# Reordering the start-up, the linear-memory path and the recurrent path of a two-path attention kernel

## The chip, the cores and the metric

The kernel runs on one core of one Trainium2 chip. The metric is the device time of one execution in microseconds. A run whose matmul clock is low throughout and whose time is more than 1.5% above the fastest of the same kernel counts as slow and is left out of every comparison; there is one such run here, the profiled one of `after_again` (1854.24 us at a mean clock of 0.707).

The engines are named as the profile names them: PE (matmuls), PEld (PE's weight loads), DVE (vector engine), ACT (activation engine), POOL, SP (here it only issues DMAs).

## The reference

Two attention paths read the same `x` (2048 x 512, bf16) and a sigmoid gate mixes them.

```python
def _A_ref(x, mem0, Wq, Wk, Wv, Wo, seg_len):      # 32 heads of 128, seg_len 32, memory of 8 rows
    mem = mem0
    for s in range(S // seg_len):                  # 64 segments, one after the other
        h = concat([mem, x[segment s]])            # 40 rows
        q, k, v = h @ Wq, h @ Wk, h @ Wv           # per head
        p = softmax(mask(q k^T * scale))
        o = (p v) @ Wo
        mem = o[:, :8]; outs.append(o[:, 8:])      # the memory feeds the next segment

def _B_ref(x, wq, wk, wv, wo, beta):               # 32 heads of 16, 4 blocks of 512 rows
    for s in range(4):
        a_dot = softmax(causal(q k^T * scale)) v
        a_mem = (phi(q) M) / (phi(q) z + 1e-6)     # phi(t) = t+1 if t > 0 else exp(t)
        o = g * a_mem + (1 - g) * a_dot            # g = sigmoid(beta), one number per head
        M += phi(k)^T v; z += sum(phi(k))
    return o @ wo

g = sigmoid((x * gate_w).sum(-1))
return g * _A_ref(...) + (1 - g) * _B_ref(...)
```

## The kernel before

The kernel records operations with what they read and write, per engine, and turns the dependences into semaphore waits. Each engine is given its own list, in the recorded order, and the order in which operations are planned is what this change alters. Three parts run one after the other: start-up, path B, path A.

Start-up: four weight loads share one semaphore group, and DVE pads wq and wk ahead of the evictions of the transposed x.

```python
        P.dma(g_bw, ... wqN_sb ...); P.dma(g_bw, ... wkN_sb ...); P.dma(g_bw, ... wvB_sb ...)   # [cut]
        for nat, pad, rn, rp in ((wqN_sb, wqB_sb, "wqN", "wqB"), (wkN_sb, wkB_sb, "wkN", "wkB")):
            P.op("dve", ... dv.memset(pad[:], 0.0) ...)
            for c in range(C):
                P.op("dve", ... dv.tensor_copy(pad[...][:, :, 0:DH], nat[...]) ...)
    P.dma(g_bw, ... woB_sb ...)
    # [cut] transposes of x on PE, each evicted to xT by DVE
```

Path B works on groups of 4 heads, 8 groups in each of 4 blocks. A group has 10 score tiles per head in three waves ("w"; 4, 4 and 2 tiles), each followed by exponentials on ACT; the K, Q, V projections and phi(K) ("pKr") of the next group are put in between, and PV ("p"), the linear memory's numerator ("nz"), its update ("mz") and a DVE chain that mixes both belong to the group before.

```python
        seq = []                                # order in one pass of the loop over groups, before
        if havew: seq.append(("w", 0))
        if havep: seq.append(("mz", None)); seq.append(("p", qc_parts[0]))
        if haven: seq.append(("pK", None))
        if havew and NW > 1: seq.append(("w", 1))
        if havep and len(qc_parts) > 1: seq.append(("p", qc_parts[1]))
        if haven: seq.append(("pQ", None))
        # [cut] ("w", 2)
        if havep: seq.append(("nz", None))
        if haven: seq.append(("pV", None))
        if havep: seq.append(("chain", None))
        if haven: seq.append(("pKr", None))
        # [cut]
    # phi(K): PE product -> DVE kmin -> ACT kexp -> DVE phik; kp, projQ and mz share PSUM bank 7
    # chain, blocks 1 to 3: rd, ad, dm, rm, am, df = am-ad, dg = df*g, o = ad+dg   (8 DVE operations)
```

Path A, one segment: K and Q projections, scores, exponentials, mask, normalisation, V projection, transposes of P, PV, Wo.

```python
    # at the start of segment s: the memory, from the bank of the last Wo (behind the eviction "atx" of aT)
        P.op("dve", lambda dv: dv.tensor_copy(hTc[:, :, SEG:L], src), reads=[rbank[6]], writes=[rm], name="hm%d" % s)
    # [cut] K, Q (evicted by ACT), scores
    tr_after = {4: 0, 6: 1, 7: 2}               # P transposes of head groups 0, 1, 2 after V groups 4, 6, 7
    # [cut] groups 0 and 1 transpose into bank 0, group 2 into bank 1
    pend = v["A_pending_tail"]
    if pend:                                    # every fourth segment: 4 transposes of aT, 4 B-row matmuls
        plan_group_tail_pe(pend[0], ...)
    P.op("dve", ... PT_sb[0:L, 0:24 * L] <- bank 0 ...)
    P.op("dve", ... PT_sb[0:L, 24 * L:H * L] <- bank 1 ...)
    # [cut]
    vres = [Rs("V_sb%d" % j) for j in range(NVC)]
    for b, (h0, h1) in enumerate(HG):           # PV: every group waits for all of V
        P.op("pe", f_pv, reads=vres + ptres, writes=[rbank[b]], ...)
        P.op("act", ... OT_sb[...] <- bank b ...)
    # [cut] Wo, then atx
```

The softmax here doesn't subtract the row's maximum and nothing guards it: scores larger than these inputs give would overflow.

## Time and profile before

| | before |
|---|---|
| median of 5 runs (range) | 1854.98 us (1848.8 to 1857.86) |
| span of the profiled run, mean granted clock | 1853.8 us, 0.884 |
| first projection of path B (start of its weight load) | 31.1 us |
| period per group, blocks 0 / 1 and 2 / 3 | 8.4 (6.9 to 9.7) / 13.9 / 10.1 us |
| path A, mean period of a segment | 22.19 us |

A period is the distance between the same instruction in neighbouring passes, read from the timeline (for block 0 the eviction of V).

The table by stretches of the kernel before; the stretches are the start-up, blocks 0 to 3 of path B (cut at each block's first projection), the stretch that waits for Wv and Wo, and path A from its first Wo matmul on. Columns: stretch, its length, busy time and count of PE, PEld, DVE, ACT and POOL, then granted clock, DMA share, GB/s.

```profile
0.00:31.10 31.10, 8.60 (x133) 7.95 (x134) 13.02 (x30) 1.92 (x4) 3.67 (x12) 0.76 0.94 351
31.10:109.00 77.90, 52.29 (x1091) 32.91 (x1107) 36.97 (x100) 46.08 (x105) 20.30 (x32) 0.78 0.06 24
109.00:221.00 112.00, 64.80 (x1219) 42.21 (x1233) 58.55 (x159) 49.32 (x112) 20.30 (x32) 0.62 0.01 2
221.00:333.40 112.40, 64.70 (x1219) 41.64 (x1233) 58.27 (x158) 49.29 (x112) 20.30 (x32) 0.62 0.01 2
333.40:422.00 88.60, 57.30 (x962) 33.97 (x974) 48.84 (x112) 46.81 (x104) 21.23 (x34) 0.63 0.01 1
422.00:447.19 25.19, 20.48 (x384) 14.56 (x385) 5.17 (x12) 10.11 (x19) 2.09 (x4) 0.79 0.95 335
447.19:1853.80 1406.61, 1325.83 (x32496) 1016.42 (x32512) 375.54 (x852) 666.12 (x1262) 117.60 (x250) 0.95 0.02 5
```

In blocks 1 and 2 no engine is busy more than 58% of the time, so they are bound by waits. In path A PE is busy 94%.

The waits of the kernel before: who waited for whom, microseconds in total, times, longest.

```profile
ACT Kmin L545 <- DVE Kmin L543: 76.1, 24, 5.0
...
PE pb L634 <- DVE phiKg L547: 52.4, 21, 3.3
...
PE pb L618 <- DVE phiQ L508: 38.4, 18, 2.3
...
PE pb L796 <- DVE hT L785: 30.4, 63, 0.5
```

The first line is the key to path B. The timeline of one group of block 2 shows it (start, length, engine, line, operation, and in brackets the idle time before it and what ended it):

```profile
248.13 0.43 DVE L675 TENSOR_TENSOR orow<-adot,dtmp 128x256 bf16<-128x256 f32 x1
248.48 0.42 DVE L543 TENSOR_SCALAR Kmin<-pb 128x256 bf16<-128x256 f32 x1
248.93 0.42 ACT L545 ACTIVATE Kmin<-Kmin 128x256 bf16<-128x256 bf16 x1 [4.52 <-DVE Kmin L543]
...
249.25 2.04 ACT L580 ACTIVATE PT_g<-pb 128x512 bf16<-128x512 f32 x4
```

The score matmuls of this wave started at 245.92 and took 0.64 us, so their exponentials (L580) could have begun near 246.6. They began at 249.25, because on ACT they stand behind the phi(K) exponential (L545), whose input DVE makes only after the chain that ends with L675. In these lines ACT did not start the ready exponentials ahead of the waiting operation: of the 4.52 us in which it stood idle, about 2.3 passed with them ready behind it (246.6 to 248.93).

In path A the interesting place lies between V and Wo. The chain of waits of one segment of the kernel before (start, length, what):

```profile
...
1044.18 0.60 ACT V_sb L868
...
1044.83 0.48 PE pb L894 x12
...
1045.39 0.58 ACT OT_sb L899
...
1046.02 4.35 PE pb L908 x128
...
1050.39 0.29 DVE aT_st L914
1050.68 0.11 DVE hT L785
...
1050.84 1.17 PE pb L796 x40
```

PV (L894) waits for the last V eviction on ACT; Wo (L908) waits for the first PV eviction; the next segment's K (L796) waits for two DVE operations, of which only the second makes its input. Wo takes 4.35 us here and 3.4 to 3.6 us in segments without half clock. The difference is the clock, by half-microsecond stretches of the same segment:

```profile
1046.50:1047.00 0.50, 0.50 (x20) 0.50 (x20) 0.00 (x0) 0.25 (x1) 0.00 (x0) 1.00 0.00 0
1047.00:1047.50 0.50, 0.50 (x24) 0.50 (x20) 0.00 (x0) 0.00 (x0) 0.00 (x0) 0.66 0.00 0
1047.50:1048.00 0.50, 0.50 (x21) 0.50 (x18) 0.00 (x0) 0.00 (x0) 0.00 (x0) 0.50 0.00 0
...
1050.50:1051.00 0.50, 0.16 (x7) 0.17 (x7) 0.28 (x2) 0.00 (x0) 0.00 (x0) 0.93 0.00 0
```

From 1047.15 to 1050.57 the granted clock (third number from the end) is 0.50. The numbers in brackets count every matmul that is under way in a stretch, so they don't show the pace; the starts do: of two Wo matmuls in a row, the second starts 25 ns after the first at full clock and 33 ns at half clock (medians of this trace). This spell lasts 3.4 us. In stretches of half a microsecond, path A has 40 such spells.

### The profile page before, as it was taken

How to read it: one execution, taken by the hardware profiler on the slowest of the kernel's cores; microseconds unless marked ns; L12 is line 12 of the kernel's file. 1: busy time of each engine (PE TensorE's matmuls, PEld its weight loads, DVE VectorE, ACT ScalarE, POOL GpSimd, SP SyncE). 2: the span in 40 equal slices, each digit the busy share in tenths (PEclk: the TensorE clock that was granted, in tenths of full speed). 3: DMA queues.
4: the chain of work that ended last, by engine and by line, in shares of the span. 5: the costliest groups of instructions: out<-in, count | busy, mean ns of one | idle time of the engine just before them, and what ended most of it. 6: DMA issues, size and time to landing. Idle time of an engine off the chain costs nothing.

```text
span 1853.8 us, 80285 instructions
## 1 busy us (share of the span) xinstructions
PE 1594.0 (86%) x37501; PEld 1189.7 (64%) x37573; DVE 596.3 (32%) x1417; ACT 869.6 (47%) x1716; POOL 205.5 (11%) x396
## 2 busy tenths in 40 slices
PE   4756555668999999999999999999999999999998
PEld 3433333336777777777777777777777777777776
DVE  4454554552222222222223222222222222222222
ACT  2644344453445444444444444444444544444444
POOL 1312112220000000000010000000000100000000
PEclk7866666668999999999999999999999999999999
DMA  7000000005000000000000000000000000000000
GB/s 273 2 2 2 2 2 1 2 1 184 3 6 3 6 3 6 3 6 3 6 3 6 3 6 3 6 6 3 6 3 6 3 6 3 6 3 6 4 6 6
DMA packets 12917, 28.23 MB, mean 15 GB/s; under 512 B 800, under 2 KB 11048, under 8 KB 11048
## 3 DMA queue, kind: packets, MB, share of 16 engines
q1 hardware_dynamic: 12584, 23.09, 3.4%
q8 instruction: 294, 4.82, 1.1%
q14 instruction: 39, 0.32, 0.1%
HBM read 20.99 MB, written 2.10 MB: 12 GB/s over the span
## 4 chain that ended last, share of the span: by engine, by line
PE 69%; ACT 3%; DVE 3%; issue 1%; SPq 1%; DMA 1%; ACTq 0%
PE pb L864 24%; PE pb L796 22%; PE pb L908 14%; PE pb L814 3%; PE pb L851 3%; ACT V_sb L868 2%; ACT OT_sb L899 1%; PE pb L894 1%; DVE aT_st L914 1%; PE pb L936 1%; DVE t_sb L944 1%; DVE fin L948 1%; DMA Wo_sb<-in_A_Wo_dram 1%; SPq L310 1%; DVE hT L785 0%
## 5 line engine op out<-in xcount | busy, mean ns | idle before, releaser
L864 PE MATMUL pb<-Wv_sb,hT 128*40 128x512 bf16 x2048 | 486.9, 380 | 0.4 <-DMA Wv_sb<-in_A_Wv_dram 0.4
L868 ACT ACTIVATE V_sb<-pb 40x512 bf16<-40x512 f32 x512 | 302.0, 590 | 193.2 <-PE pb L864 180.1
L864 PEld LDWEIGHTS pb<-Wv_sb,hT 128*40 128x40 bf16 x2048 | 184.5, 99 | 184.2 <-issue 1.9
L801 ACT ACTIVATE KT_sb<-pb 128x480 bf16<-128x480 f32 (+1 forms) x192 | 101.0, 526 | 402.6 <-PE pb L796 402.6
L827 DVE TENSOR_REDUCE rsum<-P_sb 40x12 f32<-40x480 bf16 (+1 forms) x192 | 112.0, 583 | 544.6 <-POOL P_sb L822 544.6
L908 PE MATMUL pb<-OT_sb,Wo_sb 128*128 128x40 bf16 x8192 | 253.6, 189 | 22.8 <-DVE fin L948 12.2
L908 PEld LDWEIGHTS pb<-OT_sb,Wo_sb 128*128 128x128 bf16 x8192 | 243.5, 102 | 32.5 <-ACT OT_sb L899 29.0
L796 PE MATMUL pb<-hT,Wk_sb 128*128 128x40 bf16 x8192 | 218.1, 180 | 31.9 <-DVE hT L785 30.4
L796 PEld LDWEIGHTS pb<-hT,Wk_sb 128*128 128x128 bf16 x8192 | 211.6, 96 | 39.0 <-DVE hT L785 37.2
L796 PE MATMUL pb<-hT,Wq_sb 128*128 128x40 bf16 x8192 | 216.4, 180 | 2.0 <-issue 1.8
L796 PEld LDWEIGHTS pb<-hT,Wq_sb 128*128 128x128 bf16 x8192 | 210.4, 96 | 2.6 <-issue 2.3
L822 POOL TENSOR_SCALAR_AFFINE_SELECT P_sb<-P_sb 32x384 bf16<-32x384 bf16 (+1 forms) x192 | 101.5, 540 | 931.3 <-ACT P_sb L819 930.9
L580 ACT ACTIVATE PT_g<-pb 128x512 bf16<-128x512 f32 (+1 forms) x384 | 169.8, 528 | 59.1 <-PE pb L571 58.2
L801 ACT ACTIVATE QT_sb<-pb 128x480 bf16<-128x480 f32 (+1 forms) x192 | 100.8, 526 | 107.7 <-PE pb L796 107.7
L832 DVE TENSOR_TENSOR Pn_sb<-P_sb,rrec 40x480 bf16<-40x480 bf16 (+1 forms) x192 | 126.7, 660 | 6.6
L914 DVE CAST aT_st<-pb 128x128 bf16<-128x128 f32 x64 | 18.6, 291 | 320.9 <-PE pb L908 320.9
L586 POOL TENSOR_SCALAR_AFFINE_SELECT PT_g<-PT_g 128x512 bf16<-128x512 bf16 x128 | 81.6, 638 | 327.9 <-ACT PT_g L580 325.7
L851 PEld LDWEIGHTS pb<-ident,Pn_sb 40*40 40x40 bf16 x2048 | 63.5, 93 | 80.9 <-issue 27.4
L899 ACT ACTIVATE OT_sb<-pb 128x480 bf16<-128x480 f32 (+1 forms) x192 | 87.2, 527 | 48.8 <-PE pb L894 48.8
L819 ACT ACTIVATE P_sb<-pb 40x480 bf16<-40x480 f32 (+1 forms) x192 | 92.5, 511 | 2.8 <-PE pb L814 2.5
L851 PE MATMUL pb<-ident,Pn_sb 40*40 40x40 bf16 x2048 | 83.7, 178 | 0.0
L894 PE MATMUL pb<-PT_sb,V_sb 40*128 40x40 bf16 x2048 | 62.5, 177 | 21.6 <-ACT V_sb L868 21.6
(85 smaller groups left out, 1069.9 us busy)
## 6 DMA issues: line engine op xcount, KB each, us to landing
Wk_sb<-in_A_Wk_dram SPq DMA_DIRECT2D x4, 1024.0 KB, 11.6
Wq_sb<-in_A_Wq_dram SPq DMA_DIRECT2D x4, 1024.0 KB, 20.1
Wv_sb<-in_A_Wv_dram SPq DMA_DIRECT2D x4, 1024.0 KB, 9.4
Wo_sb<-in_A_Wo_dram SPq DMA_DIRECT2D x4, 1024.0 KB, 14.1
x_sb<-in_A_x_dram SPq DMA_DIRECT2D x4, 512.0 KB, 5.5
out_dram<-fin SPq DMA_DIRECT2D x16, 128.0 KB, 1.7
wqN_sb<-in_B_wq_dram SPq DMA_DIRECT2D x1, 512.0 KB, 7.4
wkN_sb<-in_B_wk_dram SPq DMA_DIRECT2D x1, 512.0 KB, 8.5
```

The source lines that it names most:

```text
L580: P.op("act", (lambda j=j: (lambda a: a.activation(ptb[:, j, 128 * n0:128 * (n0 + len(wv))], pb[j][:, 0:128 * len(wv)], ACT.Exp, scale=SCA ...
L796: ins = pe.matmul(pb[bnk][:, (h - h0) * L:(h - h0 + 1) * L], wsb[:, c, h * E:(h + 1) * E], hTc[:, c, :], start=(c == 0), stop=(c == C - 1))
L801: P.op("act", (lambda bnk=bnk, dst=dst, h0=h0, h1=h1: (lambda a: a.activation(dst[:, h0 * L:h1 * L], pb[bnk][:, 0:(h1 - h0) * L], ACT.Copy ...
L819: P.op("act", (lambda b=b, h0=h0, h1=h1, nh=nh: (lambda a: a.activation(P_sb[0:L, h0:h1, :], pb[b][0:L, 0:nh * L].rearrange("p (h k) -> p ...
L822: P.op("gp", (lambda h0=h0, h1=h1, nh=nh: (lambda g: g.affine_select(P_sb[0:SEG, h0:h1, 0:SEG], P_sb[0:SEG, h0:h1, 0:SEG], [[0, nh], [-1, ...
L827: P.op("dve", (lambda h0=h0, h1=h1: (lambda dv: dv.tensor_reduce(rsum[0:L, h0:h1], P_sb[0:L, h0:h1, :], AX.X, ALU.add)))(), reads=[rP], wr ...
L832: P.op("dve", (lambda h0=h0, h1=h1, nh=nh: (lambda dv: dv.tensor_tensor(Pn_sb[0:L, h0:h1, :], P_sb[0:L, h0:h1, :], rrec[0:L, h0:h1].unsque ...
L851: ins = pe.transpose(dst, Pn_sb[0:L, h, :], ident[0:L, 0:L])
L864: ins = pe.matmul(pb[vb][0:L, 0:512], hTc[:, c, :], Wv_sb[:, c, 512 * j:512 * (j + 1)], start=(c == 0), stop=(c == C - 1))
L868: P.op("act", (lambda vb=vb, j=j: (lambda a: a.activation(V_sb[0:L, 512 * j:512 * (j + 1)], pb[vb][0:L, 0:512], ACT.Copy)))(), reads=[rban ...
L899: P.op("act", (lambda b=b, h0=h0, h1=h1: (lambda a: a.activation(OT_sb[:, h0 * L:h1 * L], pb[b][:, 0:(h1 - h0) * L], ACT.Copy)))(), reads= ...
L908: ins = pe.matmul(pb[6][:, c * L:(c + 1) * L], Wo_sb[:, h, c * 128:(c + 1) * 128], OT_sb[:, h * L:(h + 1) * L], start=(h == 0), stop=(h == ...
```

## The change

Its intent: begin path B earlier; take the wait of the phi(K) exponential out of ACT's queue and shorten the DVE chain; let PE run through from V to Wo; bring the memory forward; hide the B-row matmuls. The core of the diff:

```diff
 # start-up: one semaphore per weight; ACT copies each half (no zeroing), DVE is left to evict x
-        P.dma(g_bw, ... wqN_sb ...)
+        P.dma(P.group("bwq"), ... wqN_sb ...)            # wk and wv likewise
-            P.op("dve", ... dv.memset(pad[:], 0.0) ...)
-                P.op("dve", ... dv.tensor_copy(pad[...][:, :, 0:DH], nat[...]) ...)
+                for half in range(2):
+                    P.op("act", ... a.activation(pad[...][:, :, half * DH:(half + 1) * DH], nat[...], ACT.Copy) ...)
 # path B: order of one pass
         w 0
-        mz(g-1); p(g-1) first half
+        pKr(g+1)
         pK(g+1)
         w 1
-        p(g-1) second half
+        nz(g-1)
         pQ(g+1)
+        p(g-1) first half
         w 2
-        nz(g-1)
+        p(g-1) second half
         pV(g+1)
+        mz(g)
         chain(g-1)
-        pKr(g+1)
 # path B: the chain. The factors g and 1-g go into the 128x16 reciprocals
-   rd, ad, dm, rm, am, df = am-ad, dg = df*g, o = ad+dg
+   rd, rdg = rd*(1-g), ad, dm, rm, rmg = rm*g, am, o = ad+am
 # path A
+    plan_brow_piece(s, ...)                              # one B-row matmul per segment, ahead of K
+    if s % 4 == 0 and s >= 4:                            # tail: transposes of aT at the segment's start
+        plan_group_tail_atr(...); plan_group_tail_dve(...)
-            Q evicted by ACT
+            Q evicted by DVE
-    tr_after = {4: 0, 6: 1, 7: 2}                        # into banks 0, 0, 1; two evictions, after all
+    transposes into banks 0, 1, 2, each evicted at once: group 0 after V group 4, 1 after V, 2 after PV 0
-        P.op("pe", f_pv, reads=vres + ptres, ...)
+        P.op("pe", f_pv, reads=vres[h0 // 4:(h1 + 3) // 4] + [Rs("PT_sbg%d" % b)], ...)
+    the memory's eviction (hm) planned at the end of the segment, ahead of atx
```

## The prediction

> **What bounds it now.** Stage table: start-up 0-31 us, path B 31-424, weight loads 424-447, path A (64 recurrent segments) 447-1854. In A PE is busy 94%, granted clock 0.95; a segment takes 22.2 us on average (first projection to next, in the chain of waits), so A is PE-bound with small bubbles. B is latency-bound: PE busy 57-67%, DVE 48-56%, ACT 41-58%, clock 0.60-0.77. Timeline, period per head group: 9.5 us in block 0, 13.9 in blocks 1 and 2, 10.1 in block 3. Waits: PE on phiKg 52 us, on phiQ 38 us, all in B.
>
> **Start-up.** Before, DVE waits until 16.5 us for four weight loads that share one semaphore, and the transposed-x evictions queue behind it (21.1-28.4). After, x is evicted from about 10 us; sixteen ACT copies (about 0.57 each, estimated from ACT's 128x512 times) finish near 20.5, where projections begin instead of 31.1. Gain about 10.
>
> **B.** Why 13.9: the phi(K) exponential precedes the next logit exponentials on ACT, and its input waits behind the 3 us DVE chain. So ACT stands idle 4.6 us (wait table: 76 us in all). [...] The change moves phi(K) a group ahead, behind wave 0; mz comes an iteration later; nz moves away from phiQ. It also drops two 0.42 us DVE operations per group for two small ones. The new loop that I see: chain 2.4, kmin, kexp, phik 1.4, Q projection 1.8, evQ/qmin/qexp/phiq 2.5, vev and mzup 1.3: about 9.5 us in blocks 1 and 2; new, Q must wait for phik (same bank). Block 3 about 8.4, block 0 about 8.3, PE-limited at half clock. With fill and drain: 5 + 27 + 27 + 12 = about 71 saved.
>
> **A.** (1) The memory eviction goes ahead of aT: projection starts about 0.2 us earlier. (2) Before, P transposes share two banks and all of PV waits for both evictions and the last V eviction; between V and Wo, waits of about 1 us. With a bank per head group, PV0 follows directly and transpose 2 is filled in. I count third-group Wo starting about 0.75 us earlier after V6. (3) The tail of every fourth segment costs 1.28 us; its B-row matmuls now go one per segment into the wait for the memory, the transposes remain (0.5 us). (4) Q evictions to DVE (0.65 each) are off the path. Together 1.2 us per segment. (5) After the thin stretch the clock drops to 0.5 for 3.4 us in about two thirds of segments, and Wo takes 4.3 instead of 3.5 us[...]. Fewer bubbles should remove some: 0.15 more. 63 x 1.35 = 85 saved. The 23 us weight load stays.
>
> **Predicted:** 1855 - 10 - 71 - 85 = 1688 us, range 1640 to 1740; faster 0.97, within 2% 0.025, slower 0.005.
>
> **Right if:** first projection near 20 us; blocks 1 and 2 at 9-10 us per group, PE waits on phiKg gone; A at 20.6-21.1 us per segment, PE's wait for hT about 0.25 us. **Wrong if:** the bank that kp, Q and mz share serializes B (waits of Q projection on phiKg, of kp on MZ), keeping blocks 1 and 2 above 11; half-clock spells in A stay or grow (clock below 0.95); PV waits on the new P-transpose evictions as long as before; ACT copies land late. [...]

## The result, and the profile after

| | before | after |
|---|---|---|
| median (range) | 1854.98 us | 1689.79 us (1688.1 to 1696.65, 8 runs) |
| ratio of fast runs | | 0.9117, 95% interval 0.9102 to 0.9132 |
| span, mean clock of the profiled run | 1853.8, 0.884 | 1691.5, 0.947 |
| first projection of path B (start of its weight load) | 31.1 | 24.3 |
| period per group, blocks 0 / 1 and 2 / 3 | 8.4 / 13.9 / 10.1 | 7.4 (the last four 7.15) / 9.0 / 7.4 to 8.7 |
| path A, mean period of a segment | 22.19 | 20.98 |

A ratio is the mean time of one kernel's fast runs over that of the other's in the same rounds, so it is not quite the ratio of the medians.

The same table by stretches, kernel after:

```profile
0.00:24.30 24.30, 7.99 (x133) 7.75 (x134) 7.23 (x20) 13.24 (x21) 3.67 (x12) 0.85 0.93 332
24.30:94.20 69.90, 48.22 (x1097) 32.02 (x1107) 33.46 (x100) 46.15 (x105) 20.29 (x32) 0.87 0.17 67
94.20:177.00 82.80, 55.24 (x1225) 37.55 (x1233) 55.58 (x159) 49.42 (x112) 21.02 (x32) 0.79 0.01 2
177.00:259.50 82.50, 54.72 (x1225) 37.22 (x1233) 55.44 (x158) 49.42 (x112) 20.96 (x32) 0.79 0.01 2
259.50:338.00 78.50, 51.50 (x1025) 33.47 (x1031) 43.99 (x111) 46.81 (x104) 20.82 (x34) 0.74 0.02 6
338.00:361.15 23.15, 17.73 (x333) 12.26 (x330) 7.11 (x15) 9.21 (x17) 1.87 (x4) 0.85 0.97 350
361.15:1691.50 1330.35, 1291.95 (x32448) 1006.90 (x32512) 493.14 (x1104) 573.35 (x1071) 117.07 (x250) 0.99 0.02 5
```

Subtracting stretch from stretch: start-up 6.8 us less, blocks 8.0, 29.2, 29.9 and 10.1, the stretch of the weight loads 2.0, path A 76.3; together 162.3, the difference of the spans. The clock rose in every stretch; how much of path B's gain is the clock's, and how much the shorter waits', no run here separates.

The waits of the kernel after. The wait of mz on phi(K) (L634 before, L635 now) is gone from the list, and so is that of nz on phi(Q); smaller ones have come in: Q's projection waits for phi(K), because both use bank 7 (12.8 us), and phi(K)'s product waits for the update of M by mz (6.6 us in 15 waits).

```profile
ACT Kmin L546 <- DVE Kmin L544: 19.6, 13, 4.5
...
PE pb L798 <- DVE hT L918: 13.7, 48, 0.3
...
PE pb L495 <- DVE phiKg L548: 12.8, 16, 1.3
...
```

The timeline of one group of block 1, kernel after: the score exponentials (L581) now go first, and the phi(K) exponential waits for its input while ACT has only 0.80 us of idle time.

```profile
133.30 2.06 ACT L581 ACTIVATE PT_g<-pb 128x512 bf16<-128x512 f32 x4 [0.86 <-PE pb L572]
...
136.17 0.42 ACT L546 ACTIVATE Kmin<-Kmin 128x256 bf16<-128x256 bf16 x1 [0.80 <-DVE Kmin L544]
```

The chain of waits of one segment of path A, kernel after, from the end of V (left out) on: transposes (L855), PV (L894) and Wo (L909) follow each other on PE with 0.10 us between them (the line "issue"), and one DVE operation separates Wo from the next K (L798).

```profile
...
905.19 0.40 PE pb L855 x12
905.59 0.40 PE pb L894 x12
906.00 0.30 PE pb L855 x8
906.29 0.40 PE pb L894 x12
906.70 0.10 issue
906.79 0.35 PE pb L894 x8
907.15 4.16 PE pb L909 x128
...
911.33 0.20 DVE hT L918
...
911.58 0.44 PE pb L798 x11
```

Half-clock time in path A fell from 137 us in 40 spells to 34 us in 10. The lines that explain the start-up are shown with the experiment `start2`.

### The profile page after: what moved, and what is told of

It is laid out like the page before. It is cut to its first block, busy times and chain, and to the rows that moved or that the text cites. A ratio compares the mean times of both kernels' runs of the same rounds, so it can differ in the third digit from the quotient of the medians.

```text
span 1691.5 us, 80368 instructions
## 1 busy us (share of the span) xinstructions
PE 1527.4 (90%) x37477; PEld 1167.2 (69%) x37573; DVE 695.9 (41%) x1663; ACT 787.6 (47%) x1541; POOL 205.7 (12%) x396
## 4 chain that ended last, share of the span: by engine, by line
PE 76%; issue 1%; DVE 1%; SPq 1%; DMA 1%; ACT 0%; ACTq 0%
PE pb L870 26%; PE pb L798 25%; PE pb L909 13%; PE pb L894 4%; PE pb L855 4%; PE pb L821 3%; DVE hT L918 1%; DMA Wo_sb<-in_A_Wo_dram 1%; SPq L310 1%; PE pb L935 0%; DVE aT_st L920 0%; SPq L304 0%; ACT OT_sb L898 0%; DVE fin L981 0%; DVE t_sb L977 0%
## 5 line engine op out<-in xcount | busy, mean ns | idle before, releaser
L870 PE MATMUL pb<-Wv_sb,hT 128*40 128x512 bf16 x2048 | 474.9, 380 | 1.1 <-DMA Wv_sb<-in_A_Wv_dram 0.7
L870 PEld LDWEIGHTS pb<-Wv_sb,hT 128*40 128x40 bf16 x2048 | 189.4, 99 | 197.1 <-issue 1.3
L808 DVE CAST QT_sb<-pb 128x480 bf16<-128x480 f32 (+1 forms) x192 | 115.6, 602 | 326.0 <-PE pb L798 318.4
L909 PE MATMUL pb<-OT_sb,Wo_sb 128*128 128x40 bf16 x8192 | 230.3, 182 | 2.6 <-issue 1.2
L798 PE MATMUL pb<-hT,Wk_sb 128*128 128x40 bf16 x8192 | 218.3, 180 | 15.3 <-DVE hT L918 13.7
L909 PEld LDWEIGHTS pb<-OT_sb,Wo_sb 128*128 128x128 bf16 x8192 | 222.6, 97 | 5.9 <-issue 1.9
L798 PEld LDWEIGHTS pb<-hT,Wk_sb 128*128 128x128 bf16 x8192 | 212.1, 96 | 19.8 <-DVE hT L918 17.5
L798 PE MATMUL pb<-hT,Wq_sb 128*128 128x40 bf16 x8192 | 218.2, 180 | 4.9 <-issue 4.3
L798 PEld LDWEIGHTS pb<-hT,Wq_sb 128*128 128x128 bf16 x8192 | 211.1, 96 | 6.7 <-issue 6.2
L581 ACT ACTIVATE PT_g<-pb 128x512 bf16<-128x512 f32 (+1 forms) x384 | 170.1, 529 | 38.7 <-PE pb L572 37.2
L861 DVE COPY PT_sb<-pb 40x480 bf16<-40x480 bf16 (+1 forms) x192 | 70.9, 369 | 165.9 <-PE pb L855 165.9
L918 DVE CAST hT<-pb 128x32 bf16<-128x32 f32 x63 | 12.0, 191 | 259.1 <-PE pb L909 259.1
L898 ACT ACTIVATE OT_sb<-pb 128x480 bf16<-128x480 f32 (+1 forms) x192 | 94.0, 524 | 22.2 <-PE pb L894 13.4
L855 PEld LDWEIGHTS pb<-ident,Pn_sb 40*40 40x40 bf16 x2048 | 63.6, 93 | 56.3 <-issue 27.4
L894 PE MATMUL pb<-PT_sb,V_sb 40*128 40x40 bf16 x2048 | 82.8, 178 | 6.2
```

The source lines that it names most:

```text
L581: P.op("act", (lambda j=j: (lambda a: a.activation(ptb[:, j, 128 * n0:128 * (n0 + len(wv))], pb[j][:, 0:128 * len(wv)], ACT.Exp, scale=SCA ...
L798: ins = pe.matmul(pb[bnk][:, (h - h0) * L:(h - h0 + 1) * L], wsb[:, c, h * E:(h + 1) * E], hTc[:, c, :], start=(c == 0), stop=(c == C - 1))
L808: P.op("dve", (lambda bnk=bnk, dst=dst, h0=h0, h1=h1: (lambda dv: dv.tensor_copy(dst[:, h0 * L:h1 * L], pb[bnk][:, 0:(h1 - h0) * L])))(), ...
L855: ins = pe.transpose(dst, Pn_sb[0:L, h, :], ident[0:L, 0:L])
L870: ins = pe.matmul(pb[vb][0:L, 0:512], hTc[:, c, :], Wv_sb[:, c, 512 * j:512 * (j + 1)], start=(c == 0), stop=(c == C - 1))
L894: ins = pe.matmul(pb[b][:, (h - h0) * L:(h - h0 + 1) * L], V_sb[0:L, h * E:(h + 1) * E], PT_sb[0:L, h * L:(h + 1) * L], start=True, stop=True)
```

## The experiments

All twelve kernels gave correct results. Times that I call gains are (1 - ratio) x 1855 us. "A in the trace" is the time from the first Wo matmul to PE's last instruction: 1402.9 us before, 1327.1 after. Three edits add one part of the change to the kernel before (`start_only`, `b_order`, `b_fuse`), one adds all of path A's part (`a_all`); the others undo or extend the full change.

### start_only

```diff
 kernel before
+ the start-up of the full change (own semaphores, ACT copies), nothing else
```

> The kernel before with the start-up part of the change alone. Theory: the three parts of the kernel run one after the other and share no engine time, so this part alone gives what the start of the full change shows, first projection at about 24.3 us instead of 31.1, and the run is about 7 us faster (5 to 9). Rival: part of the 10 us that I predicted is lost to something else in the full change, and alone this part gives 10 us.

Measured: 1846.96 us median, ratio 0.9942 (0.9915 to 0.9968), a gain of 11 us with an interval of 6 to 16. The trace is sharper: the first projection's matmul starts at 24.69 us as in the full change (31.50 before), and path A's first Wo matmul at 440.32 instead of 447.19, 6.9 us earlier. The theory stands; the interval of the times alone would not have told 7 from 10.

### b_order and b_fuse

```diff
 b_order: kernel before
+ the new order of one pass in path B (the list in the diff above); the chain stays the old one
 b_fuse: kernel before
+ the new chain, the order stays the old one
```

> The kernel before with the new order of work in path B alone; the chain of DVE operations is the old one. Theory: what cost time was the order (phi(K) behind the DVE chain, ahead of the next logit exponentials on ACT), so 60 to 75 us of path B's 79 come from this alone, with blocks 1 and 2 at about 9.5 us per group. Rival: the DVE load was the limit, and the order alone gives less than 40 us.

> The kernel before with the shorter DVE chain alone; the order of work is the old one. Theory: in blocks 1 and 2 the chain lies in the loop, so each group gains the net of about 0.45 us, 16 x 0.45 = 7 us, with blocks 0 and 3 some 8 to 12 us in all. Rival (DVE load is the limit): 30 us or more.

Measured: `b_order` 1788.32 us, ratio 0.9625 (0.9606 to 0.9643), a gain of 70 us, with a mean period of 10.2 us in block 1 (119.86 to 170.72 in five periods). `b_fuse` 1845.38 us, ratio 0.9934 (0.9913 to 0.9954), a gain of 12 us; its period in block 1 is 13.4 us. In the traces, path A's first Wo matmul comes 65.4 and 9.2 us earlier than before. So the order was most of it, as the theory says, and DVE load as such was not: the same chain, cut by half a microsecond, gave just that half microsecond per group. Block 1's period with the order alone, 10.2, was longer than my 9.5 and the full change's 9.0, so the shorter chain is worth more after the reordering than before it.

### a_all

```diff
 kernel before
+ all of path A's part of the change, nothing else
```

> The kernel before with all of path A's part of the change and nothing else. Theory: A alone gives the 76 us that the trace of the full change shows there (72 to 80). Rival: A gains part of it from what the other parts leave behind [...], and alone it gives under 70 us.

Measured: 1779.09 us, ratio 0.9577 (0.9555 to 0.9598), a gain of 79 us. A in the trace is 1320.2 us, 82.7 less than before. The four gains sum to 11 + 70 + 12 + 79 = 172 us; the full change gained 164. The trace gives 82.7, a little above the 72 to 80 that I expected, and the rival (under 70) is out. Within the intervals the four gains add up. That does not make the parts independent: in block 1 the shorter chain took 0.5 us off a period in the old order and 1.2 us in the new one (10.2 to 9.0).

### pv_old and pv_old_fill

```diff
 pv_old: full change
- transposes into three banks, evicted one by one, PV group by group
+ the old arrangement (two banks, two evictions, all of PV waits for both and for all of V)
 pv_old_fill: pv_old
+ def f_fill(pe): n matmuls pe.matmul(pb[6][:, 160:256], ident, Wq_sb[:, 0, 96*k:96*(k+1)])   # read by nobody
+ 3 of them ahead of the last P transpose, 8 ahead of PV, 4 ahead of Wo
```

> The full change with the old arrangement of the P transposes, of PV and of their evictions put back (two shared banks, all of PV waits for everything). Theory: it loses the 0.73 us per segment that I read between the sixth V group and the third Wo group, 47 us, and the clock's half-speed spells come back (mean clock in A from 0.99 to about 0.95), another 15 to 20: 60 to 70 us slower than the full change, about 1752 us. Rival: the spells don't hang on this gap, and the loss is about 47 us at an unchanged clock.

> As pv_old, with 15 small matmuls per segment (128x96, into a part of a bank that nothing reads, results thrown away) put where PE waits: 3 before the last P transpose, 8 before PV, 4 before Wo. They do no useful work. Theory: the half-speed spells come from PE being thinly used in that stretch, so busy-work lifts the clock in A (to 0.97 or more) and the run is 5 to 15 us faster than pv_old, though more work is done and the waits are the same. Rival: the spells come from something else (the waits for the memory, or the small transposes as such): the clock stays at pv_old's and the run is as long or 5 to 10 us longer.

Measured: `pv_old` 1753.59 us, ratio 0.9444 (0.9413 to 0.9474), 61 us slower than the full change; `pv_old_fill` 1736.71 us, ratio 0.9362 (0.934 to 0.9384), 15 us faster than `pv_old`. The table by stretches for path A, first `pv_old`, then `pv_old_fill`:

```profile
363.21:1749.14 1385.93, 1334.89 (x32512) 1016.49 (x32512) 488.03 (x1040) 567.49 (x1072) 116.29 (x250) 0.95 0.02 5
```

```profile
362.89:1732.01 1369.12, 1355.98 (x33457) 1032.41 (x33457) 487.20 (x1040) 567.75 (x1073) 117.18 (x250) 1.00 0.02 5
```

With 945 more matmuls recorded, path A is 16.8 us shorter. The clock is the only thing that improved: 41 half-speed spells with 140 us became none. The stretch from PV to Wo did not get shorter, as the timeline of one segment shows, PE alone, first `pv_old`, then `pv_old_fill`. From the start of PV (L900, L911) to the start of Wo (L914, L926) both need 1.19 us; only Wo is shorter.

```profile
887.98 0.97 PE L900 MATMUL pb<-PT_sb,V_sb 40*128 40x40 bf16 x32 [0.44 <-ACT V_sb L875]
889.17 4.41 PE L914 MATMUL pb<-OT_sb,Wo_sb 128*128 128x40 bf16 x128 [0.21 <-ACT OT_sb L905]
```

```profile
904.22 0.98 PE L911 MATMUL pb<-PT_sb,V_sb 40*128 40x40 bf16 x32
...
905.41 3.60 PE L926 MATMUL pb<-OT_sb,Wo_sb 128*128 128x40 bf16 x128
```

The filler is not free. In segments at full clock without pauses, PV starts 1.29 us after the last V matmul starts, against 1.12 in `pv_old`, and the shortest segment is 21.38 us against 21.21: 0.17 us per segment, 11 us in 63 (an estimate). So 16.8 us is what remains of the clock's gain after the filler's own cost; the 140 us at half clock cost about 28 (an estimate).

So the 59 us that `pv_old` loses in path A against the full change are two things. Waiting proper is about 43 us: the shortest segment, at full clock in both, is 21.21 us in `pv_old` and 20.53 in the full change, and 63 x 0.68 = 43 (I had read 47 from one segment). The other 16 are mainly the clock, 140 us at half clock against 34. The rivals, that the clock does not hang on this gap or that the small transposes alone bring the spells, are out: with the filler the same transposes are there and no spell is.

### hm_late

```diff
 full change
- hm (memory into the next hT), then atx (aT)
+ atx, then hm
```

> The full change with the eviction of the memory put behind that of aT again. Theory: PE waits for hT 0.48 instead of 0.28 us in the 48 segments without a tail; in the tail segments the transposes wait for aT in any case: about 10 us slower than the full change. Rival: the wait is covered by the B-row matmul now, and nothing is lost (under 3 us).

Measured: 1702.99 us, ratio 0.9179 (0.9153 to 0.9206), some 11 us slower than the full change by the ratios (9 against `after_again`, below). In the trace path A is 6.8 us longer (1333.9); the first Wo matmul also comes 3.6 us later, which the edit can't cause. The shortest segment of the trace is 20.73 us instead of 20.53, exactly the 0.2 us by which the two DVE starts differ. The theory stands, and the B-row matmul does not cover the wait.

### q_on_act

```diff
 full change
- Q evicted by DVE
+ Q evicted by ACT, as before
```

> The full change with the Q evictions back on ACT. Theory: off the path in A, where neither engine is near full: within 3 us of the full change. Rival: on ACT they hold up the exponentials, and it is 5 to 15 us slower.

Measured: 1697.58 us, ratio 0.9152 (0.913 to 0.9173). Against the full change's 0.9117 (0.9102 to 0.9132) this is 6 us, and the intervals just overlap. In the trace path A is unchanged (1328.1 us against 1327.1, shortest segment 20.53 in both), and the first Wo matmul comes 2.8 us later although the edit touches nothing ahead of path A. I count no cost in path A as shown, and the 6 us as undecided.

### after_again and brow_lump

```diff
 after_again: the full change
 brow_lump: full change
-    plan_brow_piece(s, ...)                  # one B-row matmul per segment
+    plan_brow_flush(s // 4 - 1, ...)         # four in one lump, ahead of the tail's transposes
```

> The full change once more, beside the others on the same chip. The question is what varies: path A took 76 us less in the full change's trace but 83 us less with A's part alone, and the trace of the full change has 14 pauses of PE with no cause shown. If they are chance, A is between 1320 and 1330 us here and the time within 0.3% of the earlier 1690.

> The full change with the four B-row matmuls of a group in one lump ahead of the tail's transposes. Theory: single, they hide in the wait for the memory; in a lump of about 0.9 us they exceed the tail's wait of 0.5 us by 0.4 to 0.6, in 16 segments: 6 to 10 us slower than the full change. Rival: a single one costs about as much as it does in the lump, and the time is the same within 3 us.

Measured: `after_again` 1693.4 us, ratio 0.913 (0.9109 to 0.9152), both from its four fast runs (1690.63 to 1694.9). Its profiled run was the slow one, 1854.24 us at a mean clock of 0.707, so its trace answers nothing about the pauses in path A; the times do repeat within 0.3%. That run is told of again in the last section.

`brow_lump` 1697.73 us, ratio 0.9152 (0.9127 to 0.9177): 4 us above `after_again` of the same rounds, intervals overlapping. My 6 to 10 were too much. The timeline of a tail of the full change, and then of `brow_lump`, tells why:

```profile
597.42 0.40 PE L935 MATMUL pb<-ident,aT_st 128*128 128x128 bf16 x4 [0.48 <-DVE aT_st L920]
```

```profile
602.40 1.02 PE L968 MATMUL pb<-woB_sb,oT 128*128 128x512 bf16 x4
603.26 0.39 PE L935 MATMUL pb<-ident,aT_st 128*128 128x128 bf16 x4
```

In segments at full clock without pauses, a tail costs 1.1 us in the kernel before (22.52 us against 21.43), 0.44 in the full change and 0.65 in `brow_lump`. In the full change the last Wo weights had been passed at 596.76 (the weight load of the B-row matmul starts there), so the transposes wait 0.66 us in all. The lump needs 0.86 (602.40 to 603.26). That is 0.2 us per tail, 3 us in 16. The tail's gain therefore came from moving it into the wait for the memory; cutting its matmuls into single ones added little, and less than the times resolve.

### start2

```diff
 full change
-   x: one semaphore for four loads               +   one for each load
-   16 ACT copies                                 +   POOL zeroes, 4 copies on ACT (wq), 4 on DVE (wk)
-   initial memory evicted through bank 6, behind the gate's ACT and DVE operations
+   initial memory evicted through bank 7; sigmoid(z) as 1/(1+exp(-z)), so one ACT table
-   gate computed in the start-up                 +   gate computed at the start of path A
```

> The full change with a shorter start-up: x waited for in four pieces, padding zeroed by POOL so that half the copies remain, wk's copies on DVE, the gate computed at the start of path A, sigmoids from the exponential so that no second table is loaded, the initial memory evicted through another bank. Theory: my 20.5 us for the first projection failed because the copies took 0.66 us and because the projection waits, by its bank, for the initial memory, which stands behind the gate, its table load and all copies; with this chain gone, the first projection starts at 15 to 17 us instead of 24.3, and the run is 6 to 10 us faster than the full change. Rival: the copies alone bind: 19 us or later and less than 4 us gained.

First the lines of the full change's start-up that the theory rests on, from its timeline:

```profile
17.02 5.24 ACT L385 ACTIVATE wkB_sb<-wkN_sb 128x512 bf16<-128x512 bf16 x8
...
22.28 1.28 ACT L437 ACT_TABLE_LOAD   x1
...
24.00 0.17 DVE L452 COPY memT<-pb 128x32 bf16<-128x32 bf16 x1
...
24.69 1.49 PE L481 MATMUL pb<-xT,wkB_sb 128*128 128x512 bf16 x3 [4.78 <-DVE memT L452]
```

The copies end at 22.26. Then come a table load of 1.28 us, the gate's sigmoid, two DVE operations and the eviction of the initial memory from bank 6 (L452), into which the first projection writes. Up to the first projections the trace of the full change has three table loads of 1.28 us (at 0.80, 22.28 and 23.89), that of `start2` one (at 12.39).

Measured: 1688.02 us, ratio 0.9103 (0.9082 to 0.9123), 5 us faster than `after_again` of the same rounds (the intervals overlap; its trace is 4.0 us shorter). The first projection's weight load starts at 15.25 us, 9.0 earlier, and its matmul at 15.26, 9.4 earlier. That is the expected size, and the rival (the copies alone bind, 19 us or later) is out; but as `start2` also lets x start earlier (first transpose at 4.95 us instead of 9.37), it does not tell how the 9 us divide.

Of the 9.4 us the trace has 2.95 left at the first Wo matmul (358.20 against 361.15). About 3.1 were given back where I moved the gate: from the last transposes of path B to the first K projection of path A the full change needs 3.24 us (332.88 to 336.12), `start2` 6.31 (326.14 to 332.45). I had taken this place for free because Wv and Wo are still being loaded. K and Q do not wait for these loads; in the full change V waits 0.66 us and Wo 1.01 for them, so little of the gate's time could be hidden. Another 2.7 us went in path B, which took longer from its first projection to its last transposes (310.9 us against 308.2); why is open. The last 0.7 went between K and Wo.

### best

```diff
 start2
-   four DVE operations of 16 partitions update M      +   one of 128 partitions
-   tail's transposes ahead of K                       +   behind Q
-   Wv loaded after path B                             +   in memory of its own, loaded during path B
```

> start2 and three more: one DVE operation for the memory update instead of four (about 0.6 us per group in the DVE loop of blocks 0 to 2), the tail's transposes after K and Q instead of in the wait for the memory, Wv loaded during path B. Estimates from the traces: 9 + 8 + 4 + 5: about 26 us faster than the full change, some 1664 us. If less, then the DVE loop isn't what bounds blocks 1 and 2 any more.

Measured: 1671.22 us, ratio 0.9008 (0.8986 to 0.903), 22.6 us faster than `after_again` (26 expected) and 9.9% faster than the kernel before. It beats both kernels. By stretches of its trace: the periods of blocks 1 and 2 fell from 9.0 to 8.1 us (78.4 and 79.0 us per block), so the DVE loop did bind them; A in the trace is 1322.0 us, 5 less than after; from the last transposes of path B to the first Wo matmul it needs 30.1 us against 32.1 in `start2`, 2 us less instead of the 5 that I expected from the early load of Wv. In neither trace does a matmul of this stretch wait for a load; what differs is the two pauses of PE (3.8 us together against 4.9) and 16 of the V matmuls (4.35 us at a mean clock of 0.83, against 5.14 at 0.70). That the early load brought these is not shown.

## Why the prediction was right

The time on record was 1688 and the measured median 1689.8. The mechanisms were right in the main, but an agreement within 2 us is luck: against the traces the terms are off by -3 (start-up), +6 (path B), -9 (path A) and +2 us (weight loads), and these errors cancel.

1. **Start-up, 10 predicted, 6.8 in the trace.** The step that failed is "sixteen ACT copies ... finish near 20.5, where projections begin". A copy took 0.63 us busy and 0.66 in sequence, not 0.57, so they ended at 22.3; and the projection waited 2 us more for the eviction of the initial memory, which stood behind the gate on ACT and DVE. I had not followed who reads bank 6. `start2` removed both, and the late start of x, and started at 15.26.
2. **Path B, 71 predicted, 77 in the trace.** The mechanism holds: the wait of ACT fell from 76.1 to 19.6 us, PE's waits on phi(K) of mz and on phi(Q) are gone, and the order alone gave 70 us by its times (65 in its trace) against 12 (9) for the shorter chain. The wait that I named as new, Q's projection on phi(K), came, with 12.8 us. The mis-sized term is block 0, "about 8.3, PE-limited at half clock": its last four periods took 7.15 us each, at a granted clock of 1.00, and the mean of all seven is 7.4. The 9.5 us before was misread too: it holds for the last periods of the block, while the mean of seven is 8.4 (two at a clock of 1.00 took 6.9 and 8.1). So the two errors partly cancelled, and block 0 gave 8 us instead of 5. Blocks 1 and 2 gave 59 instead of 54, with a period of 9.0 instead of 9.5; block 3 gave 10 instead of 12.
3. **Path A, 85 predicted, 76 in the trace of the full change, 83 in that of `a_all`.** Each size was seen: the memory's eviction 0.2 us per segment (`hm_late`), the new arrangement of PV 0.7 and less half-clock time (`pv_old`, `pv_old_fill`), Q evictions off the path in the trace. The shortest segment is 20.53 us. What keeps the mean at 20.98 is half clock in some segments, the tails (0.44 us every fourth segment), and short pauses of PE that the profile marks "issue", with no releaser: in the full change's trace 14 of over 0.25 us, 5.9 us together, against one of 0.3 us before. In the nine other traces that I counted there are 6 (`b_order`) to 14 (`pv_old_fill`), 9 in `a_all`, so they do not go with one part of the change. `a_all` has both less half clock (20.5 us in 6 spells, against 34 in 10) and fewer pauses (4.2 us together); by the rate of `pv_old_fill` that is about 4 of the 7 us between it and the full change, an estimate.

   What the pauses go with can be read from the traces, though I had not looked. Each of the 128 pauses of over 0.25 us in path A, in all 14 traces together, ends 1.2 to 1.6 us after a packet of the DMA queue that the profile calls "instruction" (q8) has landed. In the full change, for example, a packet landed at 469.17 and the pause of 470.16 ends at 470.62. Such packets, 16 KB each, come some four times in a segment (256 in path A of the full change), and only 8% of path A's matmuls start at such a distance from one. So the pauses go with the packets of this queue. Whether the packets cause them, and why only 14 of the 256 come with one, is open; no run was made to test it.
4. **The clock.** I had written that fewer bubbles should remove some half-clock spells, 0.15 us per segment, 9 us. Half-clock time in A fell by 103 us. In the trace of the kernel before, a Wo matmul starts 33.7 ns after the one ahead of it in the spells and 26.8 ns outside them (means); if all of the 103 us were spent on matmuls of this kind, that would be 103 x (1 - 26.8 / 33.7) = 21 us. `pv_old_fill` measured 16.8 for removing 140, or about 28 without the filler's own cost, which for 103 gives 20. Both are estimates. This is about twice what I predicted, and it offset the pauses.
5. **"The 23 us weight load stays"** holds within 2 us (25.2 before, 23.2 after).

## What to carry to other kernels

Look in an engine's list for an operation whose input comes from a long chain elsewhere, and put the ready work ahead of it; here that was worth six times as much as shortening the chain (70 us against 12). In path A a short sparse stretch on PE cost twice, once as waiting (about 43 of the 59 us that `pv_old` loses there) and once as the half-clock spell after it (most of the other 16); cheap filler matmuls told the two costs apart, once the time that the filler itself takes was measured too (0.17 us per segment). Before calling a stretch free for moved work, check that what runs there truly waits for the thing you think it waits for, and before timing a first instruction, follow the last reader of the bank that it writes.

## Half-clock spells, a slow run and pauses, as measured

- In path A of the kernel before, half-clock spells followed a stretch whose longest PE wait was 0.44 us (0.81 us in segments with a tail), with small transposes and 40-row matmuls between the waits: 40 spells in 63 segments, and 41 in `pv_old`. Fifteen 128x96 matmuls in that stretch brought them to none (`pv_old_fill`). How much filler that takes, and what part the transposes have in the spells, no run here isolates.
- The slow run of `after_again`, on one core, shows a granted clock of 0.75 in each of the 60 half-microsecond stretches that I read in path A, and 0.73 on the mean of path A, spells of half clock included (119 us), with 1854.2 us instead of about 1693. No cause was found.
- For the Wo matmuls of 40 columns in the trace of the kernel before, the median from start to start is 33 ns in the spells (granted clock 0.50) and 25 ns at full clock. So at half clock these matmuls were a third slower, not twice as slow.
- The pauses of PE without a releaser ("issue") took 0.26 to 0.65 us, 14 in path A of the full change's trace, and 1.0 and 2.6 us in the stretch of its weight loads (with 1.4 and 1.5 us from the landing of a q8 packet to the end of the pause).
